# A bias table made in one fp32 matmul and one exponential, with first queries and keys ahead on SyncE's queue and every band row on it

## The chip, the cores and the metric

The kernel runs on one core of a Trainium2 chip. The metric is the device time of one execution in microseconds (us), the median of several runs. Engines are named as the profile names them: PE multiplies matrices, DVE and ACT do elementwise work (ACT also the exponentials), POOL and SP here issue transfers; PEld is PE's weight load.

## The reference

Attention with a learned bias by relative position, for 8 batches, 8 heads, 576 positions and 64 features, followed by a bilinear feed-forward layer over the 4608 tokens:

```
scores = q @ k.T / 8
n = abs(i - j)
bucket = n if n < 16 else min(31, 16 + int(log(n/16)/log(8) * 15))
scores += bias_table[bucket]          # 32 buckets x 8 heads
x = softmax(scores) @ v               # heads side by side: 4608 x 512
out = ((x @ w_a) * (x @ w_b)) @ w_out # 512 -> 1536 -> 512
```

Everything comes in and goes out in fp32.

## The kernel before

**The bias as a factor.** Softmax is unchanged when one value is subtracted from all scores of a head, so the kernel works with exp(bias − bias of the last bucket), which is 1 wherever two positions are at least 128 apart. The table in memory, `tab`, holds 1088 such factors for each head. It is filled with ones, and its middle 256 entries come from one matmul: `oh_sb`, a one-hot matrix of 32 buckets by 256 distances, against `eb_sb`, the exponentials of the differences in bf16 (line 250, after a subtraction on DVE in line 240). DVE copies the product into `tab_sb` (line 258) and SP sends it to `tab` (line 266). From there the band rows are read back as tiles, row after row shifted by one place: `W_sb` for each pair of heads, in two column parts (tokens `W0` to `W3` for columns from 320 on, `R0` to `R3` for the rest, line 261), and `Wt_sb` for the tail rows (`Wta`, `Wtb`). `W0` is issued by SP, the others by POOL. After its exponential each score tile is multiplied by its band on DVE (lines 470, 444, 539, 531).

**Pairs and stages.** Two heads make a pair; there are 32 pairs, four in each batch. 576 positions are four blocks of 128 and a tail of 64. For the first two batches (pairs 0 to 7) q and k are transposed on PE (lines 330, 339, 370) and copied out of PSUM to `QT`, `KT` and `ZB`; pairs 0 to 3 have their scores made in halves (line 455, `S`) with exponentials on ACT (line 461, `E`) and products on DVE (line 470, `M`). Later pairs use transposing transfers. `AV` are the products with v (lines 568, 572, 578), `N` their normalisation (lines 589 to 596), `X` the transposes of the result. Feed-forward units (`FA`, `FB`, `FO`: lines 642, 649, 652, 679) are put between them.

**The order.** The order in the opening, through the first feed-forward chunk, is a list of tokens written out by hand: `<` names are loads, `w2` is two filler matmuls on zeros, and the ending `:A` or `:D` says whether ACT or DVE does a copy or a padding. Every engine and every queue works through its instructions in this order. From pair 8 on a loop sets the order, which is the same for all the rest.

**The head.** Ahead of the list SP issues the constant `cn_sb` (one-hot matrix and identity), then q and k of the first pair in fp32 (`load_first`, line 226) into `kq32`, a part of `xn_sb` that is free until then. ACT issues two small loads of the bias table. The tokens `YQ` and `YK` turn the two fp32 pieces into bf16. POOL issues the other loads, which change the type on the way: `q123h0` is the first half of the positions of pairs 1 to 3, `q123h1` the second, `v0` and `v1` the values, `tq` and `tk` the tails of q and k, `vta` and `vtb` those of v, `wa0`, `wb0` and so on the weights.

```
nc.sync.dma_start(out=tab.ap(), in_=tab_sb[0:H, :])
...
load_w(int(name[1]), *((320, NY) if name[0] == "W" else (0, 320)), nc.sync if name in ('W0',) else nc.gpsimd)
```

Of the kernel before, what the change touches and what calls it, by code (L numbers as in the profile page):

```python
# [13 lines left out]
def kernel(  # L14
# [24 lines left out]
    NT = B * S  # L39
# [150 lines left out]
    def pad_z(b, hh):  # L190
        nc.vector.memset(ZB[b][64 * hh:64 * hh + 64, :, :, Dh - Dh * hh:128 - Dh * hh], 0.0)
# [45 lines left out]
    nc.vector.memset(tab_sb.bitcast(FP32)[0:H, :], TWO_ONES)  # L237
    pad_ones(0)
    pad_ones(1)
    nc.vector.tensor_tensor(out=bt_sb[0:NB, :], in0=bt_sb[0:NB, :], in1=bl_sb[0:NB, :],  # L240
                            op=mybir.AluOpType.subtract)
    warm = ps_av.tile([128, 512], FP32, tag="av", name="warm")

    def warm_up(n, dst=None):
        for _ in range(n):
            nc.tensor.matmul(out=(warm if dst is None else dst)[:, :], lhsT=zero_sb[:, 0:128],
                             rhs=zero_sb[:, :], start=True, stop=True)
# [12 lines left out]
    def load_w(hp, y0, y1, eng):  # L260
        eng.dma_start(out=W_sb[hp][:, :, y0:y1],
# [21 lines left out]
    def load(name):  # L283
        if name[0] in "qk" and name[1:2].isdigit():
            ps, _, half = name[1:].partition("h")
            p0, n = int(ps[0]), len(ps)
            if half:
                load_qh(2 * p0, 2 * p0 + 2 * n, int(half))
            else:
                b, h = divmod(2 * p0, H)  # L290
                (load_q if name[0] == "q" else load_k)(b, h, h + 2 * n)
        elif name[0] in "tu":
            load_compact(int(name[0] == "u"), int(name[1] == "k"))
        elif name in ("v0", "v1"):
            load_v(0, 4 * int(name[1]), 4 * int(name[1]) + 4)
        elif name[:3] == "vb1":
            load_v(1, *((0, 4) if name[3] == "a" else (4, 8)))
        elif name[:2] == "vt":
            load_vt_part(int(name[2] == "1"), "ab".index(name[-1]))
        elif name == "wo":  # L300
            load_w_out()
        elif name[:2] == "Wt":
            load_wt("ab".index(name[2]))
        elif name[0] in "WR":
            load_w(int(name[1]), *((320, NY) if name[0] == "W" else (0, 320)), nc.sync if name in ('W0',) else nc.gpsimd)
        else:
            load_weights(*((moe_w_a, wa_sb) if name[1] == "a" else (moe_w_b, wb_sb)), int(name[2]))

# [418 lines left out]
    def v_next(s):  # L727
# [7 lines left out]
    ACT = nc.scalar  # L735

    opening = """
        <q123h0 <k1 <tk <vtb <k23 <W1 <W0 <v0 <vta <tq <W2 <W3 <v1 <Wta <q123h1 <R0 <Wtb <R1 <k4 <wa0
        <wb0 <R2 <uq <q5 <q4 <R3 <k5 <wa1 <q7 <wb1 <k6 <uk <k7 <vb1a <vb1b <vt1a <q6 <wb2 <vt1b <wa2 <wo
        PC0:A PX0:D YQ0:A PC1:A PU0:D PV0:A PX1:D TQ0 YK0:D TK0 CQ00:A CQ01:D CK0:D TQ10 PF1:A CQ10:D  # L740
        S000 E000 PV1:D S001 E001 TK1 CK1:D TQ30 TZ1 CZ1:D S011 CQ30:D E011 S101 TQ20 CQ20:D E101 M101
        S100 E100 TK3 CK3:D KS EK M000 TK2 S301 E301 CK2:D w2 S200 E200 M100 M001 w1 S201 E201 V0:D
        PU1:D w2 S300 E300 M200 M201 AV00 TZ0 AV10 S010 CZ0:A N00 T0 N10 E010 X10 X00 CX00:A V1:D AV20
        CX10:A TQ11 TQ21 M301 M300 ET0 AV30 CQ11:A S110 CQ21:A N20 M010 M011 PW:A MT0 S111 TQ31 E110 X20
        CQ31:A E111 T1 ET1 N30 M110 X30 CX20:D CX30:D AV01 T2 TK4 M111 S210 ET2 E210 FA0a HA0a N01 T3
        MT1 X01 AV11 CK4:D CX01:A PF0:D LH ET3 N11 S211 E211 FB0a FA1a HA1a X11 G0a MT2 CX11:D S310 E310
        FB1a G1a S311 M210 FA2a FB2a HA2a E311 TQ5 TQ4 CQ4:A M211 FA3a AV21 CQ5:A S42 G2a S43 FB3a TZ0x
        MT3 M311 HA3a M310 TK5 E42 N21 FA4a HA4a CZ0x:D AV31 LV CK5:D X21 E43 TQ7 CQ7:A G3a N31 S41 E41
        S52 E52 FB4a FA5a HA5a CX21:D G4a M43 TK6 X31 CX31:D FB5a S40 E40 CK6:D S53 G5a FA0b HA0b TZ1x
        M41 CZ1x:D FB0b G0b S51 E53 FA1b HA1b TK7 FB1b FA2b E51 M52 HA2b CK7:D S50 G1b V2:D FB2b FA3b  # L750
        E50 V3:D G2b HA3b T4 M40 FB3b G3b S70 M42 ET4 MT4 FA4b FB4b T5 HA4b M53 E70 G4b TQ6 ET5 M51
        CQ6:A AV40 N40 FA5b S71 E71 S73 MT5 M50 FB5b HA5b AV41 S72 E73 G5b N41 M71 FA6f M73 T6 E72 M72
        ET6 MT6 AV50 FB6f HA6f N50 S62 S61 E62 G6f M62 FA7f HA7f AV51 N51 TH S60 E61 M61 FB7f G7f E60
        M60 S63 E63 FA8f HA8f T7 ET7 M63 M70 FB8f G8f AV60 FA9f FB9f N60 MT7 AV70 HA9f G9f FA10f HA10f
        FB10f N70 AV71 G10f FA11f HA11f FB11f N71 X71 AV61 X70 FO00 G11f N61 FO01 FO02 CX71:D CX70:D HO0
    """

    h0 = (0, 1)
# [2 lines left out]
    def step(token):  # L761
# [72 lines left out]
            tr_x(p, jqs)  # L834
        elif kind == "CX":
            copy_x(p, jqs, eng)
        elif kind == "YK":
            copy(eng, kn[0][:, 0:512], kq32[0])
        elif kind == "YQ":
            copy(eng, qn[0][:, 0:512], kq32[1])  # L840
        elif kind == "PV":
            pad_vt(0, p, eng)
        elif kind == "PC":
# [101 lines left out]
```

The softmax here doesn't subtract the row's maximum and nothing guards it: scores larger than these inputs give would overflow.

## Time and profile before

| what | value |
|---|---|
| time, median of 3 runs | 414.17 us (413.11 to 414.28) |
| the profiled execution, and its span from first to last instruction | 413.9 us, 412.1 us |
| PE busy | 401.5 us, 97% |
| DVE, ACT, POOL busy | 58%, 61%, 32% |
| chain that ended last, PE's share | 95% |

The page gives busy time by engine and, in forty slices of the span, how full each engine was. The times of the opening are read from the timeline, which lists start, length and the idle time ahead of each group of instructions with what ended it. A line of the profile reads: engine, line of the kernel, operation, output and input. The profile's lines are those of the kernel before; in the changed kernel the same statements stand five lines further up.

### The profile page before, as it was taken

Reading aid. Unit: us, or ns where it says so; the run is one execution under the profiler, and the core shown is the slowest. Engines: PE = TensorE matmul, PEld = TensorE weight load, DVE = VectorE, ACT = ScalarE, POOL = GpSimd, SP = SyncE. Lnnn points to the kernel's source line nnn. Section 1 sums busy time; section 2 is a strip of 40 time slices with the busy share of each in tenths; the row PEclk is TensorE's granted clock in tenths of the full one; section 3 lists DMA queues with packets and bytes.
Section 4 is the critical chain, followed back from the end, with each engine's and each line's share of the span. In section 5 each row is a group of like instructions: output and inputs, shape, how many; then the busy total and the mean of one; then the engine's idle time right before and its main releaser. Section 6 shows DMA issues by size and latency. Waiting matters only on the chain.

```text
span 412.1 us, 8718 instructions
## 1 busy us (share of the span) xinstructions
PE 401.5 (97%) x3420; PEld 209.6 (51%) x3471; DVE 240.6 (58%) x568; ACT 252.0 (61%) x386; POOL 131.4 (32%) x188
## 2 busy tenths in 40 slices
PE   7999999999999999999999999999999999999996
PEld 3476656455554555455445555555445454444443
DVE  4799997366755765476646764567547652421320
ACT  5898992577748665667557765767476642322321
POOL 5966466887029400960069004300000000000000
PEclk9999999999999999999999999999999999999999
DMA  9999999999969924994199908960520012002004
GB/s 152 185 204 197 206 137 148 166 184 131 91 127 157 141 40 91 151 127 94 35 159 150 120 17 136 117 92 17 117 67 17 16 40 78 0 5 98 2 2 102
DMA packets 135962, 42.36 MB, mean 103 GB/s; under 512 B 113544, under 2 KB 131176, under 8 KB 135920
## 3 DMA queue, kind: packets, MB, share of 16 engines
q0 software_dynamic: 81120, 19.88, 54.9%
q1 hardware_dynamic: 49456, 12.61, 19.9%
q10 hardware_dynamic: 5344, 9.31, 7.1%
q8 instruction: 27, 0.44, 0.5%
q14 instruction: 15, 0.12, 0.1%
HBM read 39.23 MB, written 9.45 MB: 118 GB/s over the span
## 4 chain that ended last, share of the span: by engine, by line
PE 95%; DMA 1%; ACT 1%; issue 1%; DVE 0%; ACTq 0%; SPq 0%
PE pb L642 23%; PE pa L642 23%; PE po L679 22%; PE av L578 8%; PE qk L415 7%; PE av L568 2%; PE av L572 2%; PE qkh L455 1%; PE qkt L488 1%; DMA xn<-in_k_dram 1%; PE trb L330 1%; PE trb L424 1%; PE trk L330 1%; ACT ath L461 0%; PE qkt L494 0%
## 5 line engine op out<-in xcount | busy, mean ns | idle before, releaser
L439 ACT ACTIVATE at<-qk 128x1024 bf16<-128x1024 f32 x112 | 113.4, 1029 | 27.4 <-DMA out_dram<-ob 10.3
L652 DVE TENSOR_TENSOR g<-pb,ha 128x512 bf16<-128x512 f32 (+1 forms) x114 | 75.6, 663 | 74.8 <-PE pb L642 58.5
L642 PE MATMUL pb<-xn,wb 128*128 128x512 bf16 (+1 forms) x440 | 111.1, 368 | 0.8
L642 PE MATMUL pa<-xn,wa 128*128 128x512 bf16 (+1 forms) x440 | 110.8, 368 | 0.7
L649 ACT ACTIVATE ha<-pa 128x512 f32<-128x512 f32 (+1 forms) x114 | 66.3, 581 | 67.6 <-PE pa L642 63.8
L679 PE MATMUL po<-wo,g 128*128 128x512 bf16 x403 | 95.5, 379 | 0.8
L444 DVE TENSOR_TENSOR at<-at,W 128x1024 bf16<-128x1024 bf16 x112 | 75.0, 685 | 22.4 <-ACT at L439 22.3
L642 PEld LDWEIGHTS <-wa 128*128 128x128 bf16 x456 | 41.2, 98 | 46.6 <-issue 6.8
L642 PEld LDWEIGHTS <-wb 128*128 128x128 bf16 x456 | 40.6, 98 | 42.9 <-issue 4.7
L679 PEld LDWEIGHTS <-g 128*128 128x128 bf16 x420 | 38.8, 98 | 44.9 <-issue 2.5
L684 ACT ACTIVATE ob<-po 128x512 f32<-128x512 f32 x34 | 20.4, 600 | 40.2 <-PE po L679 30.1
L578 PE MATMUL av<-vm,at 128*128 128x65 bf16 x896 | 41.2, 193 | 0.0
L578 PEld LDWEIGHTS <-at 128*128 128x128 bf16 x896 | 37.4, 97 | 6.1
L174 POOL DMA_DIRECT2D vt<-in_v_dram x12 | 7.4, 622 | 101.9 <-PE av L572 101.1
L136 POOL DMA_DIRECT2D qn<-in_q_dram x48 | 36.6, 825 | 9.2 <-PE trb L501 6.9
L589 DVE RECIPROCAL rc<-av 128x6 f32<-128x6 f32 (+1 forms) x64 | 11.9, 186 | 45.7 <-PE av L578 41.1
L145 POOL DMA_DIRECT2D kn<-in_k_dram x48 | 36.2, 800 | 2.6 <-DMA qn<-in_q_dram 1.6
L568 PE MATMUL av<-vt,att 128*128 128x130 bf16 x152 | 33.6, 221 | 0.2
L415 PE MATMUL qk<-QB,KB 64*128 64x512 bf16 x192 | 29.1, 381 | 0.3
L591 DVE TENSOR_TENSOR XG<-av,rc 128x384 bf16<-128x384 f32 (+2 forms) x64 | 27.2, 425 | 2.2
L515 ACT ACTIVATE att<-qkt 128x640 bf16<-128x640 f32 x24 | 16.8, 701 | 13.0 <-PE qkt L489 13.0
L568 PEld LDWEIGHTS <-att 128*128 128x128 bf16 x152 | 14.9, 98 | 6.4
(105 smaller groups left out, 322.8 us busy)
## 6 DMA issues: line engine op xcount, KB each, us to landing
out_dram<-ob ACTq DMA_DIRECT2D x31, 256.0 KB, 2.9
vn<-in_v_dram POOLq DMA_DIRECT2D x16, 256.0 KB, 5.7
kn<-in_k_dram POOLq DMA_DIRECT2D x48, 64.0 KB, 4.9
qn<-in_q_dram POOLq DMA_DIRECT2D x48, 64.0 KB, 4.1
wa<-in_moe_w_a_dram POOLq DMA_DIRECT2D x3, 512.0 KB, 8.9
wb<-in_moe_w_b_dram POOLq DMA_DIRECT2D x3, 512.0 KB, 8.3
wo<-in_moe_w_out_dram POOLq DMA_DIRECT2D x1, 1536.0 KB, 15.7
xn<-XG SPq DMA_TRANSPOSE x52, 3.5
```

The lines of the kernel that those rows point to most:

```text
L136: nc.gpsimd.dma_start(out=by_tile(qn[b % 2])[:, h0 // 4, t, :, :], in_=q[b, h0:h1, 128 * t:128 * t + 128, :].transpose([1, 0, 2]))
L145: nc.gpsimd.dma_start(out=by_tile(kn[b % 2])[:, h0 // 4, t, :, :], in_=k[b, h0:h1, t:SM:NM, :].transpose([1, 0, 2]))
L415: nc.tensor.matmul(out=ps[:, hh, :], lhsT=kT[r, t, :], rhs=qT[r, :, :], start=True, stop=True)
L439: nc.scalar.activation(out=at[:, :, :], in_=ps[:, :, :], func=ACTF.Exp, scale=scale)
L444: nc.vector.tensor_tensor(out=at[:, :, :], in0=at[:, :, :], in1=w[:, :, S - 1 + t:S - 1 + t - SM:-1], op=MULT)
L568: nc.tensor.matmul(out=pav[:, slot, :, :], lhsT=weights_tail(p, jq), rhs=vt[i][:, :, hp, :], start=True, stop=True)
L578: nc.tensor.matmul(out=pav[:, slot, hh, :], lhsT=weights(p, t, hh, jq), rhs=vm[i][:, 2 * hp + hh, t, :], start=False, stop=True, skip_grou ...
L591: nc.vector.tensor_tensor(out=xg[:, jqs[0]:jqs[0] + m, :, :], in0=pav[:, 0:m, :, 0:Dh], in1=rc[:, 0:m, :].unsqueeze(3).to_broadcast([128, ...
L642: nc.tensor.matmul(out=ps[:, 0:n], lhsT=w[df // 4][:, mc, 128 * (df % 4):128 * (df % 4) + 128], rhs=xn_sb[mc][:, 512 * c + lo:512 * c + lo ...
L649: nc.scalar.activation(out=ha[:, 0:n], in_=ff["pa", df, lo][:, 0:n], func=ACTF.Copy)
L652: nc.vector.tensor_tensor(out=g_sb[df][:, lo:lo + n], in0=ff["pb", df, lo][:, 0:n], in1=ff["ha", df, lo][:, 0:n], op=MULT)
L679: nc.tensor.matmul(out=po[:, :], lhsT=g_sb[df][:, 128 * tt:128 * tt + 128], rhs=wo_sb[:, df, :], start=(df == 0), stop=(df == NDF - 1))
```

## The change

- The differences to the last bucket go into the constant: a row of −1 is added to the one-hot matrix, so that one matmul of the raw bias table in fp32 gives bias minus last bias. The one-hot part is copied to fp32 on DVE (`oh32`, in a free part of `xn_sb`).
- The exponential is taken once, of the product, on ACT, straight into `tab_sb`. The second small load, the subtraction, `eb_sb` and the two fillers behind the table matmul are gone.
- SP issues q and k of the first pair first; the constant goes second on ACT's queue. Both type changes (`YQ`, `YK`) move ahead of the list, onto DVE.
- `W0` to `W3` all go on SP's queue.
- The list of the opening is a new one: loads in another order on POOL, copies and paddings divided otherwise between ACT and DVE, products with v and their neighbours in another order, one filler more.

```diff
+    oh_np[NB - 1, :] -= 1.0
...
-    oh_sb = cn_sb[:, 0:NR]
-    bl_sb = const.tile([128, H], FP32, name="bl_sb")
-    eb_sb = const.tile([128, H], BF16, name="eb_sb")
...
+    oh32 = xn_sb[2][:, NT - 512:NT].bitcast(FP32)
...
-    nc.sync.dma_start(out=cn_sb[:, :], in_=cn_handle.ap())
     load_first(q, kq32[1])
     load_first(k, kq32[0])
     nc.scalar.dma_start(out=bt_sb[0:NB, :], in_=bias_table)
-    nc.scalar.dma_start(out=bl_sb[0:NB, :],
-                        in_=bass.AP(tensor=bias_table.tensor, offset=(NB - 1) * H,
-                                    ap=[[0, NB], [1, H]]))
+    nc.scalar.dma_start(out=cn_sb[:, :], in_=cn_handle.ap())
...
-    nc.vector.tensor_tensor(out=bt_sb[0:NB, :], in0=bt_sb[0:NB, :], in1=bl_sb[0:NB, :],
-                            op=mybir.AluOpType.subtract)
+    pad_z(0, 0)
+    pad_z(0, 1)
+    nc.vector.tensor_copy(out=oh32[0:NB, :], in_=cn_sb[0:NB, 0:NR])
...
     warm_up(5)
-    nc.scalar.activation(out=eb_sb[0:NB, :], in_=bt_sb[0:NB, :], func=ACTF.Exp)
-    nc.tensor.matmul(out=tps[0:H, 0:NR], lhsT=eb_sb[0:NB, :], rhs=oh_sb[0:NB, :],
+    nc.tensor.matmul(out=tps[0:H, 0:NR], lhsT=bt_sb[0:NB, :], rhs=oh32[0:NB, :],
                      start=True, stop=True)
-    warm_up(2)
-    pad_z(0, 0)
-    pad_z(0, 1)
-    nc.vector.tensor_copy(out=tab_sb[0:H, c0:c0 + NR], in_=tps[0:H, 0:NR])
+    nc.vector.tensor_copy(out=qn[0][:, 0:512], in_=kq32[1])
+    nc.scalar.activation(out=tab_sb[0:H, c0:c0 + NR], in_=tps[0:H, 0:NR], func=ACTF.Exp)
+    nc.vector.tensor_copy(out=kn[0][:, 0:512], in_=kq32[0])
...
-... nc.sync if name in ('W0',) else nc.gpsimd)
+... nc.sync if name in ('W0', 'W1', 'W2', 'W3') else nc.gpsimd)
```

The head of the list, before and after:

```diff
-        <q123h0 <k1 <tk <vtb <k23 <W1 <W0 <v0 <vta <tq <W2 <W3 <v1 <Wta <q123h1 <R0 <Wtb <R1 <k4 <wa0
-        <wb0 <R2 <uq <q5 <q4 <R3 <k5 <wa1 <q7 <wb1 <k6 <uk <k7 <vb1a <vb1b <vt1a <q6 <wb2 <vt1b <wa2 <wo
-        PC0:A PX0:D YQ0:A PC1:A PU0:D PV0:A PX1:D TQ0 YK0:D TK0 CQ00:A CQ01:D CK0:D TQ10 PF1:A CQ10:D
-        S000 E000 PV1:D S001 E001 TK1 CK1:D TQ30 TZ1 CZ1:D S011 CQ30:D E011 S101 TQ20 CQ20:D E101 M101
-        S100 E100 TK3 CK3:D KS EK M000 TK2 S301 E301 CK2:D w2 S200 E200 M100 M001 w1 S201 E201 V0:D
-        PU1:D w2 S300 E300 M200 M201 AV00 TZ0 AV10 S010 CZ0:A N00 T0 N10 E010 X10 X00 CX00:A V1:D AV20
+        <q123h0 <tk <k1 <k23 <W0 <W1 <v0 <W3 <W2 <Wtb <vtb <tq <vta <q123h1 <R1 <Wta <v1 <R0 <R2 <k4
+        <wa0 <wb0 <q4 <q7 <k7 <q5 <vt1b <R3 <k5 <wa1 <uq <uk <wb1 <vb1a <vb1b <k6 <vt1a <wb2 <q6 <wa2
+        <wo PF1:D PU1:A TQ0 CQ00:A TK0 PX1:D PX0:D PU0:A PV1:D CK0:D PC0:A PF0:A CQ01:D w1 S000 E000
+        TQ10 S001 TK1 CQ10:D TZ1 E001 CK1:D S011 E011 TQ30 PV0:D S101 E101 CQ30:D CZ1:D TK3 CK3:D TK2
+        CK2:D V0:D S100 E100 TQ20 CQ20:D S301 E301 w2 S200 E200 w2 KS EK w1 S300 M101 S201 E300 TZ0
+        CZ0:A M000 E201 M100 AV10 M001 AV00 M301 TQ11 CQ11:A M200 T0 M300 N10 X10 N00 PW:D ET0 TQ31
+        CQ31:A M201 S010 E010 S110 E110 CX10:D TQ21 V1:D LH M011 X00 CX00:A M010 CQ21:A AV20 AV30 S111
```

More of the change, by code (lines that the diff above doesn't have):

```diff
@@ L304, in load @@
         elif name[0] in "WR":
-            load_w(int(name[1]), *((320, NY) if name[0] == "W" else (0, 320)), nc.sync if name in ('W0',) else nc.gpsimd)
+            load_w(int(name[1]), *((320, NY) if name[0] == "W" else (0, 320)), nc.sync if name in ('W0', 'W1', 'W2', 'W3') else nc.gpsimd)
         else:
@@ L743 @@
-        PU1:D w2 S300 E300 M200 M201 AV00 TZ0 AV10 S010 CZ0:A N00 T0 N10 E010 X10 X00 CX00:A V1:D AV20
[L744 to L752, printed above, removed]
@@ L753 @@
-        ET6 MT6 AV50 FB6f HA6f N50 S62 S61 E62 G6f M62 FA7f HA7f AV51 N51 TH S60 E61 M61 FB7f G7f E60
-        M60 S63 E63 FA8f HA8f T7 ET7 M63 M70 FB8f G8f AV60 FA9f FB9f N60 MT7 AV70 HA9f G9f FA10f HA10f
-        FB10f N70 AV71 G10f FA11f HA11f FB11f N71 X71 AV61 X70 FO00 G11f N61 FO01 FO02 CX71:D CX70:D HO0
+        <q123h0 <tk <k1 <k23 <W0 <W1 <v0 <W3 <W2 <Wtb <vtb <tq <vta <q123h1 <R1 <Wta <v1 <R0 <R2 <k4
+        <wa0 <wb0 <q4 <q7 <k7 <q5 <vt1b <R3 <k5 <wa1 <uq <uk <wb1 <vb1a <vb1b <k6 <vt1a <wb2 <q6 <wa2
@@ new lines @@
+        E111 T1 N20 X20 MT0 AV01 N30 CX20:D M110 N01 ET1 X30 MT1 TK4 M111 T2 CX30:A S210 FA0a X01 ET2
+        HA0a CX01:D FB0a E210 MT2 G0a CK4:A T3 AV11 N11 FA1a ET3 HA1a TQ4 M210 S211 E211 FB1a X11 CX11:A
+        FA2a HA2a S311 G1a CQ4:D S310 E311 FB2a MT3 FA3a HA3a E310 M211 TK5 G2a M311 TQ5 CK5:A PC1:D
+        AV21 N21 S42 M310 S43 FB3a FA4a G3a CQ5:A X21 TZ0x AV31 LV E42 CX21:D TQ7 N31 CZ0x:D HA4a FB4a
+        G4a S41 E43 M43 S52 FA5a CQ7:A TK7 E41 X31 CX31:D S40 HA5a E52 CK7:D E40 FB5a G5a V2:D FA0b HA0b
@@ new lines @@
+        S53 FB0b M42 TZ1x TK6 G0b E53 CZ1x:D M53 FA1b HA1b S51 E51 FB1b G1b FA2b M40 V3:D S50 FB2b HA2b
+        E50 G2b FA3b M41 HA3b T4 ET4 FB3b G3b S70 CK6:D MT4 FA4b FB4b T5 TQ6 AV40 HA4b M50 M52 G4b E70
+        S71 ET5 N40 FA5b FB5b MT5 CQ6:A E71 HA5b M51 AV41 N41 S72 G5b S73 E72 M72 FA6f E73 AV50 M70 M73
+        N50 S62 FB6f T6 HA6f E62 M62 ET6 FA7f HA7f G6f MT6 AV51 N51 TH S61 S60 E61 M61 E60 FB7f G7f S63
+        E63 M60 M63 FA8f M71 T7 FB8f HA8f G8f AV60 N60 ET7 MT7 FA9f HA9f FB9f G9f AV70 FA10f FB10f N70
@@ L756 @@
+        HA10f G10f AV71 FA11f FB11f HA11f N71 X71 AV61 X70 FO00 FO01 G11f FO02 N61 CX70:D CX71:D HO0
     """
@@ L836, in step @@
             copy_x(p, jqs, eng)
[L837 to L840, printed above, removed]
         elif kind == "PV":
```

## The prediction

> **What bounds the kernel now.** I read the page first. Its table of forty slices gives PE a 7 in the first slice and 9 in every one until the last.
>
> ```profile
> PE   7999999999999999999999999999999999999996
> ```
>
> So a change at the head can only win what PE loses there, and it must be kept by a PE that never pauses again. Busy PE counts pipelined ends, so I went next to the busy time by stretches, cut where the opening changes its character.
>
> ```profile
> 0.00:7.90 7.90, 5.28 (x32) 1.88 (x32) 3.95 (x19) 3.94 (x8) 3.78 (x9) 1.00 0.97 157
> 7.90:19.50 11.60, 11.09 (x117) 5.52 (x119) 8.06 (x19) 9.79 (x11) 11.04 (x16) 1.00 1.09 174
> 19.50:25.30 5.80, 5.08 (x109) 4.05 (x106) 5.44 (x15) 5.46 (x12) 4.63 (x7) 1.00 1.27 212
> 25.30:40.00 14.70, 14.70 (x227) 10.95 (x226) 13.27 (x44) 13.09 (x21) 9.49 (x13) 1.00 1.39 196
> ```
>
> The columns are PE, PEld, DVE, ACT, POOL. From 25.3 us PE has no gap (14.70 of 14.70). Before that come three stages: a start to 7.9, a stretch to 19.5 in which PE and ACT are both nearly full, and one to 25.3 in which DVE (5.44 of 5.80) and ACT (5.46) lead. The chain of waits, in order of time, names what the first two hang on:
>
> ```profile
> 1.72 4.51 DMA xn<-in_k_dram
> 6.25 0.44 DVE kn L322
> 6.73 0.68 PE trk L330 x8
> 7.43 0.44 DVE KT L322
> 7.92 1.03 PE qkh L455 x8
> ...
> 15.33 0.63 PE warm L246
> 15.96 0.54 PE qkh L455 x4
> ```
>
> The first keys' transfer alone is 4.51 us of the start; then the chain runs through PE itself, warm-up fillers included. The ACT timeline shows what PE's pace costs there:
>
> ```profile
> 8.57 1.94 ACT L461 ACTIVATE ath<-qkh 128x1024 bf16<-128x1024 f32 x2 [1.97 <-PE qkh L455]
> 10.67 2.86 ACT L461 ACTIVATE ath<-qkh 128x1024 bf16<-128x1024 f32 x3 [0.17 <-PE qkh L455]
> 13.93 1.02 ACT L480 ACTIVATE atk<-qkt 128x1024 bf16<-128x1024 f32 x1 [0.40 <-PE qkt L476]
> 16.55 2.95 ACT L461 ACTIVATE ath<-qkh 128x1024 bf16<-128x1024 f32 x3 [0.48 <-PE qkh L455]
> ```
>
> Ten exponentials of about 0.93 us fill 8.57 to 19.50 (10.93 us), 1.6 us of it idle, before scores that PE had not made.
>
> **What the Trainium skill says.** "TensorE: Matmul & The Clock Gate", Part 1, What's actually happening: the array runs at half clock until about 3.4 us of sustained work. The trace agrees in kind, though not in the waiting time: fillers of 512 columns start 0.43 us apart at 2 us, score groups still take half-rate steps (0.18 to 0.21 us for 256 columns) at 17.1, and the two fillers at 17.45 are 0.23 apart. The granted clock stands at 1.00 throughout, so it doesn't show this. "FP8 and Floating Point Precision", TensorE Precision Notes: true fp32 takes four passes. No fp32 matmul is in this trace. "DMA: Bandwidth & Descriptors", Issuing engines are not separate DMA queues: all issuers share the engines, and more of them save issue time only. The trace agrees: the q transfer landed 3.19 us after issue nearly alone, the k transfer behind it, beside POOL's loads, took 4.51.
>
> **Part 1, head of SyncE's queue: −1.0 us.** SP issued the constant at 0.74, q at 1.18, k at 1.72. Now q goes at 0.74 and k at 1.18, 0.54 earlier; the constant (96 KB) goes second on ACT's queue. From k's landing to the first exponential the trace has 8.57 − 6.23 = 2.34 us (cast 0.44, eight transposes 0.68, copy 0.44, scores to exponential 0.65, steps between). With the same 4.51 us k lands at 5.7 (gain 0.5); with q's 3.19, at 4.4. Of the three first transfers one is now on another queue, but the bytes up to the last of k are about the same, so I take 5.2: gain 1.0, bounds 0.5 and 1.3. Nothing else must lie in the way. DVE's new padding between the cast and the key copy is 0.27 + 0.11 + 0.11 + 0.28 = 0.77, as long as the transposes it waits for. ACT must do four paddings of about 0.4 and one q copy before the first exponential; from a table exponential ending near 5.0 that reaches 7.0, before the scores (7.5). The one filler ahead of the scores (0.43) lies inside the key copy.
>
> **Part 2, the table: +0.6 us, hidden.** Before: subtract 3.18, exponential 3.37, matmul 3.63, cast 4.04 to 4.45, transfer issued 4.48, seen by its waiters at 7.80. Removed: one small load, the subtract, the fold of the exponential into a bf16 operand. Added: an fp32 copy of the one-hot differences, 32x256, which waits for the constant (landed 2.16 us after issue before; now issued near 1.2, so about 3.6), about 0.3 by the 64x256 copies; the matmul, four passes, estimated from the page and half rate at 4 × 0.21 = 0.85, less if the passes are fewer (0.21); the exponential out of PSUM, about 0.35. So 3.6 + 0.3 + 0.8 + 0.35 = 5.05 against 4.48, bounds 4.5 and 5.6. PE's queue holds the q transposes behind that matmul, and DVE's the q and k casts behind the copy; both are ready only at 4.4 and 5.2, so the wait costs nothing unless the constant lands after 4.7. The two fillers that followed the table matmul are gone; they ran in idle time.
>
> **Part 3, band rows on SP.** The table is seen at 8.4; four issues of 0.39 go at 8.4, 8.8, 9.2, 9.6. By the single SP transfer of before (2.58) plus contention, the second lands at 11.4 to 12.0. The first product that needs it was at 12.64, and now stands behind two key copies, the values' copy and a q copy, at about 12.0. So nothing is lost, with little to spare. POOL issues three loads fewer (0.73 each). After five loads it still waits once for the table (3.24 before, some 3.5 now), with the v tails (which landed at 7.67 and will at about 13; the first value product needs them after 17), the q tails and the second q half behind that wait. The values now pass ahead of that wait: issued near 4.2 instead of 8.77, so their copy can run at 11 instead of 16.05, in DVE's idle time.
>
> **Part 4, the order.** In the score stretch PE is at half rate. Steps from the timeline: 0.48 a score group, 0.57 eight transposes of keys, 0.35 of a q half, 0.22 tails, 0.96 tail scores, 0.43 a filler. From the first score group through the last of this stage the new order has nine groups (4.32), three key sets (1.71), three q halves (1.05), one set of tails (0.22), the tail scores (0.96) and five fillers (2.15), 10.41 together. The old order has the same counts, with some gaps and the last group at full rate, and took 10.39 (7.92 to 18.31). The first part's 1.0 is kept: the last scores are out at 17.3 instead of 18.3.
>
> Then ACT: from the tenth exponential to the end of the second pair's last half it had 6.4 us; a copy of 0.33 and the tail-table copy of 0.42 go to DVE, the rest keeps its length. ACT ends that half at about 24.25 against 25.91, −1.65. DVE, step by step from the product that needs the eighth exponential (17.9): eight products at 0.60, four first normalisations at 0.55, three copies at 0.25 to 0.33, a tail pair at 0.56, one long normalisation at 0.98 and 0.2 for the tail table end near 25.9, or 26.5 with the one product that the old order has ahead of this point. There it was 27.70: −1.2, and −1.3 one tail pair later. DVE is the later of the two, so −1.3 is what reaches PE. After 25.3 PE has no idle; ACT receives about 1.2 us of copies more in 25 to 38, where its gaps were about 1.4. I charge nothing, bound 0.6.
>
> Sum: 412.1 − 1.3 = 410.8 of span. The three runs have a median of 414.17 (the profiled execution, 413.9, lies 1.8 above its span), so 412.9. The runs spread 1.17 us, and 0.3%, about what a measurement of this kernel can tell from no change, is 1.24.
>
> **Rivals.**
> *The clock rises earlier.* PE is closer packed from 6.9 on, so full rate may come at 13 to 14 instead of 17.4. The last six items (3.7 us) would halve; ACT's 0.93 a step then limits, and about 1.0 more is won: 411.9. Against it: PE was nearly gapless from 11.3 to 17.4 and stayed slow.
> *The gain is absorbed.* The bytes before k's last packet are the same, so k lands at 5.7; or the second band transfer lands late and holds the products on a DVE that is full from then on. Then 0.5 or less: 413.9.
> *Slower: POOL's queue behind the table.* The second q half is the fourth load behind the one that waits for the table, so issued near 11.2 (8.4 + 4 × 0.72), against 13.64 before, where it took 6.05. In the new order its transposes stand in PE's queue right after the first two value products, at about 18.8, and all later scores behind them. Four band transfers (520 KB) now share the engines with it. From a landing at 18.8 each microsecond costs one; from 21.4 (a latency of 10.2, where 8.9 is the longest seen below 30 us) the sum exceeds +1.3: 415.5.
>
> That the compiled order differs from the diff is excluded by the instruction lists of both kernels.
>
> **How the numbers follow.** Main case 0.42, of which 0.27 beyond 0.3%; earlier clock 0.23; absorbed 0.20; slower 0.13, and 0.02 for what I haven't seen. Faster 0.27 + 0.23 = 0.50; same 0.15 + 0.20 = 0.35; slower 0.15. The range runs from the earlier clock with the best landing (411.3) to the absorbed case plus half of the slower one (414.9).
>
> **What would show it.** Right: k landing near 5.2, first exponential near 7.5, table transfer issued near 5.05, last first-stage scores at 17.3, gapless PE from about 24, all later lines shifted by 1.3. Wrong: full-rate fillers before 15, PE waiting for the second q half, a first product after 12.6, or PE gaps between 25 and 40 before copies on ACT.

## The result and the profile after

The changed kernel takes 417.12 us (median of 6 runs, 416.1 to 418.91), the kernel before 413.94 (6 runs, 413.11 to 414.28): a ratio of 1.0086, 95% interval 1.0062 to 1.011. The forecast was 412.9, range 411.3 to 414.9: it had the wrong sign, by 4.2 us. The profiled execution of the changed kernel took 417.26 us, its span is 415.5 (before: 413.9 and 412.1). Ahead of the table's transfer the lines of the two kernels differ by one to four, from there on by five. Figures of single loads below are issue and landing in the trace; each comes from one profiled execution.

The page's row of slices shows it coarsely: two 9s have become 7s, in the second and third slices (10.4 to 31.2 us). The chain that ended last says more: 8% of it now is DMA and 88% PE, where PE had 95% before.

```profile
PE   7779999999999999999999999999999999999996
...
PE 88%; DMA 8%; issue 1%; POOL 1%; ACT 1%; ACTq 0%; DVE 0%
```

The busy time by stretches (PE, PEld, DVE, ACT, POOL, granted clock, DMA share, GB/s), for the same four stretches as before:

```profile
0.00:7.90 7.90, 5.67 (x36) 2.01 (x36) 4.11 (x19) 3.54 (x8) 4.06 (x9) 1.00 0.97 167
7.90:19.50 11.60, 9.36 (x114) 4.83 (x112) 8.13 (x17) 9.23 (x11) 7.55 (x12) 1.00 1.08 161
19.50:25.30 5.80, 5.43 (x116) 4.37 (x113) 5.01 (x17) 5.55 (x10) 5.59 (x8) 1.00 1.05 168
25.30:40.00 14.70, 12.87 (x198) 9.60 (x196) 11.93 (x35) 12.15 (x21) 8.37 (x12) 1.00 1.31 184
```

The start is better (5.67 of PE instead of 5.28). Then PE lacks 1.7 us up to 19.5 and 1.8 between 25.3 and 40, where it had been full. POOL, which only issues transfers, falls from 11.04 to 7.55 in the second stretch. The first `po` product, where the last step of the first feed-forward chunk begins, starts at 74.51 instead of 71.03; from there to the end both kernels need the same (340.94 and 341.07). So everything happens in the opening. What PE waited for there, longest first (total, times, longest):

```profile
PE pb L637 <- DMA wb<-in_moe_w_b_dram: 2.1, 2, 1.8
PE trb L365 <- DMA tlc<-in_q_dram: 1.3, 1, 1.3
```

Two loads, the q tails and the second weights; PE waited for no load after 7 us before. The chain of waits up to 32 us, in order of time, says why they were late:

```profile
1.23 2.93 DMA cn_sb<-cn_const
...
4.18 0.29 DVE xn L238
...
4.51 1.03 PE tab_ps L248 x2
...
5.57 0.38 ACT wo L252
...
5.97 3.71 DMA bias_tab<-wo
9.68 0.28 issue
9.96 0.62 POOL Wt L264
10.59 6.89 DMA vt<-in_v_dram
17.48 0.29 issue
17.77 0.72 POOL W L256
...
19.43 0.74 POOL wa L274
20.17 9.79 DMA wb<-in_moe_w_b_dram
```

It is the making of the table from end to end, and then POOL's queue: constant, fp32 copy, fp32 matmul, exponential (`wo` is the memory that `tab_sb` lies in), the table's transfer, POOL's load of a tail band that reads the table, then the loads behind it. POOL's timeline has both its stops, with their lengths in brackets:

```profile
4.18 0.93 POOL L126 DMA_DIRECT2D vn<-in_v_dram  x1
9.96 0.63 POOL L264 DMA_DIRECT2D Wt<-bias_tab  x1 [4.86 <-DMA bias_tab<-wo]
...
17.77 0.72 POOL L256 DMA_DIRECT2D W<-bias_tab  x1 [1.75 <-DMA vt<-in_v_dram]
```

The first stop is the wait for the table (3.24 before). The second: the issue at 17.77 follows the landing, at 17.48, of the v tails issued at 10.59, the eighth load before it; eight of POOL's loads were in flight. While SP and POOL both stood, the transfer engines ran dry. The stretch 9 to 11 us in single microseconds, last two columns DMA share and GB/s; first the changed kernel, then the kernel before, whose own dip is shorter and earlier (36 GB/s from 8.5 to 9.0 us):

```profile
9.00:10.00 1.00, 1.00 (x18) 0.51 (x16) 0.69 (x2) 0.72 (x2) 0.04 (x1) 1.00 0.14 23
10.00:11.00 1.00, 1.00 (x18) 0.53 (x18) 0.69 (x3) 1.00 (x2) 1.00 (x2) 1.00 0.13 23
```

```profile
9.00:10.00 1.00, 1.00 (x21) 0.76 (x23) 0.41 (x1) 1.00 (x2) 1.00 (x2) 1.00 0.81 191
10.00:11.00 1.00, 1.00 (x12) 0.42 (x8) 0.75 (x4) 0.83 (x2) 1.00 (x3) 1.00 0.87 110
```

Thirteen loads were then issued from 9.70 to 15.24 in one burst (the thirteen from 7.80 on took until 15.64 before), and most of them took longer: q tails 11.19 to 18.44 (before 10.14 to 14.09), v tails 10.59 to 17.48, second q half 12.48 to 19.63 (before 13.64 to 19.68), second weights 20.17 to 29.97 (before 18.33 to 26.60). ACT's timeline shows that the first part of the change did what it was meant to, and where its gain goes:

```profile
7.75 1.93 ACT L456 ACTIVATE ath<-qkh 128x1024 bf16<-128x1024 f32 x2
9.95 1.94 ACT L456 ACTIVATE ath<-qkh 128x1024 bf16<-128x1024 f32 x2 [0.28 <-PE qkh L450]
...
16.63 1.02 ACT L456 ACTIVATE ath<-qkh 128x1024 bf16<-128x1024 f32 x1
18.81 0.77 ACT L315 ACTIVATE ZB<-trb 64x256 bf16<-64x256 bf16 x2 [1.17 <-PE trb L365]
```

The first exponential is at 7.75 instead of 8.57, 0.82 ahead; the tenth ends at 20.6 instead of 19.5, behind the tails for which PE waited.

### The profile page after: what moved, and what is told of

The parts are those of the page before. It is cut to its first block, busy times and chain, and to the rows that moved or that the text cites. A ratio compares the mean times of both kernels' runs of the same rounds, so it can differ in the third digit from the quotient of the medians.

```text
span 415.5 us, 8711 instructions
## 1 busy us (share of the span) xinstructions
PE 401.2 (97%) x3420; PEld 210.0 (51%) x3471; DVE 240.8 (58%) x568; ACT 251.5 (61%) x385; POOL 129.2 (31%) x185
## 3 DMA queue, kind: packets, MB, share of 16 engines
q1 hardware_dynamic: 50128, 12.91, 19.5%
## 4 chain that ended last, share of the span: by engine, by line
PE 88%; DMA 8%; issue 1%; POOL 1%; ACT 1%; ACTq 0%; DVE 0%
PE pb L637 22%; PE pa L637 22%; PE po L674 22%; PE qk L410 7%; PE av L573 7%; DMA wb<-in_moe_w_b_dram 4%; PE av L563 2%; DMA vt<-in_v_dram 2%; PE av L567 2%; PE qkt L483 1%; DMA bias_tab<-wo 1%; DMA cn_sb<-cn_const 1%; PE trb L419 1%; POOL wa L274 0%; POOL tlc L161 0%
```

## The experiments

The theories, by their letters in the expectations. A: the table's later time stops POOL, and all loads behind it come late. B: the new list is itself too eager. C: the bands on SP crowd POOL's loads. D: the earlier first scores count for more than the table. E: the table's transfer stands in the transfer engines behind loads that POOL issued ahead of it. Ratios are to the kernel before, timed beside it on the same chip (medians there 413.26 to 413.86). A difference between two variants is one of medians, partly from different chips. "Seen" is the time at which SP issues the first band load, which waits for the table.

| kernel | edit | us (runs) | ratio (95%) | table issued, seen |
|---|---|---|---|---|
| before | | | | 4.48, 7.80 |
| after | all of it | 417.12 (6) | 1.0086 (1.0062 to 1.011) | 5.97, 9.70 |
| e1_head | new head, old list | 414.32 (14) | 1.0016 (1.0008 to 1.0025) | 6.45, 9.23 |
| e2_bands_sp | before + bands on SP | 414.76 (18) | 1.0020 (1.0005 to 1.0035) | 4.47, 8.05 |
| e3_list_only | old head, new list, bands on SP | 415.83 (6) | 1.0049 (1.0033 to 1.0064) | 4.97, 9.22 |
| e7_list_pool | old head, new list, bands on POOL | 418.39 (6) | 1.0122 (1.0102 to 1.0143) | 4.45, 8.76 |
| e8_order_only | before + order of first transfers | 416.01 (6) | 1.0050 (1.0034 to 1.0066) | 7.08, 9.36 |
| e4_late_wt | after, tail band later on POOL | 415.21 (20) | 1.0045 (1.0030 to 1.0059) | 6.04, 10.40 |
| e6_cq7 | e4, one ACT copy earlier | 415.43 (7) | 1.0051 (1.0031 to 1.0071) | 5.83, 10.73 |
| e5_cn_first | after, constant first on SP | 414.67 (15) | 1.0028 (1.0018 to 1.0037) | 5.05, 9.44 |
| e9_v0_behind | after, values behind the tail band | 417.76 (4) | 1.0099 (1.0079 to 1.0119) | 6.09, 8.30 |
| e10_tails_ahead | after, tails ahead of the tail band | 415.52 (6) | 1.0057 (1.0035 to 1.0080) | 5.91, 10.69 |
| e11_cn_v0 | e5 and e9 | 417.96 (4) | 1.0109 (1.0089 to 1.0128) | 5.06, 8.72 |
| e15_cn_v0_late | e11, values' copy later | 416.43 (6) | 1.0086 (1.0057 to 1.0115) | 5.06, 8.73 |
| e16_v0_late | e9, values' copy later | 416.96 (5) | 1.0078 (1.0063 to 1.0093) | 5.86, 8.83 |
| e12_fill | before + two fillers | 414.00 (14) | 0.9998 (0.9987 to 1.0008) | 4.45, 7.77 |
| e13_before_nowait | before, bands from a constant | 413.75 (13) | 1.0003 (0.9992 to 1.0014) | no wait |
| e14_after_nowait | after, bands from a constant | 413.88 (13) | 1.0005 (0.9995 to 1.0015) | no wait |
| e17_nowait_s41 | e14, scores moved near 37 us | 413.65 (14) | 1.0003 (0.9992 to 1.0014) | no wait |
| e18_cn_s41 | e5, the same move | 414.98 (6) | 1.0044 (1.0026 to 1.0061) | 5.05, 9.43 |

### The parts, one at a time

`e1_head` takes the new head with the old list and the old queues of the bands. `YQ0` and `YK0` go from the list, since the head does them; against the kernel before, beside the lines of the head:

```diff
-        PC0:A PX0:D YQ0:A PC1:A PU0:D PV0:A PX1:D TQ0 YK0:D TK0 CQ00:A CQ01:D CK0:D TQ10 PF1:A CQ10:D
+        PC0:A PX0:D PC1:A PU0:D PV0:A PX1:D TQ0 TK0 CQ00:A CQ01:D CK0:D TQ10 PF1:A CQ10:D
```

> The changed head alone (fp32 table, first queries and keys first, both casts on DVE) with the old list, bands on the queues of before. Theory A (the later table holds POOL's queue, and what stands behind it comes late): table transfer issued near 6.0, POOL waits 4.8 us in place of 3.2, first scores 0.8 earlier but the loads behind the wait 1.5 later; 1.0 to 2.5 us slower than before. Theory B (the new list asks for loads earlier than they can come): no slower than before, up to 0.8 faster. Theory C (four band transfers on SP crowd POOL's loads out): the same as B.

414.32: the head costs 0.5 where the list stays, between what A (1.0 to 2.5) and what B and C (nothing) expected. POOL waits 4.67 for the table, nearly the changed kernel's 4.86, yet the loads behind that wait take about as long as before (q tails 11.56 to 15.97), and PE waits for none of them. Its first exponential is at 9.37: ACT's paddings of the old list now stand behind the table's exponential (6.05).

`e2_bands_sp` is the kernel before with the four band issues on SP.

```diff
-... nc.sync if name in ('W0',) else nc.gpsimd)
+... nc.sync if name in ('W0', 'W1', 'W2', 'W3') else nc.gpsimd)
```

> The kernel before with the four band transfers on SP's queue and nothing else changed. Theory A: POOL no longer waits at the first band and issues values, v tails and q tails 3 us earlier, its wait for the table moves to the tail table when that has long landed; 0 to 1 us faster. Theory B: within 0.5 us of before. Theory C: the loads issued beside the bands take 6 to 7 us in place of 4, 1 to 3 us slower.

414.76. With no band in front, POOL runs on to the second values before it waits, for 0.81. The bands pay for it; SP's timeline, and the wait on DVE:

```profile
4.47 0.35 SPq L266 DMA_DIRECT2D bias_tab<-wo  x1
8.05 2.34 SPq L261 DMA_DIRECT2D W<-bias_tab  x4
```

```profile
DVE ath L470 <- DMA W<-bias_tab: 2.2, 1, 2.2
```

The first two bands take 6.3 us or more (landed 14.39, 15.29; W0 took 2.6 before) and the first product waits 2.2. That is Theory C turned round: the bands, not POOL's loads, are late. That POOL's freed loads crowd them is argued, not tested.

`e3_list_only` and `e7_list_pool` put the new list behind the old head (with `YQ0:D YK0:D` at its start), the one with bands on SP, the other with only `W0` there.

```diff
-        <wo PF1:D PU1:A TQ0 ...
+        <wo YQ0:D YK0:D PF1:D PU1:A TQ0 ...
```

> The new list and all bands on SP with the head of before (bf16 table, constant first on SP), both casts on DVE at the head of the list. Theory A: table transfer issued at 4.5, POOL's wait about 3.3, the wait for the q tails falls from 1.3 to 0 and that for the second weights from 1.8 to below 0.5; 2 to 3.5 us faster than the changed kernel, about the time of before. Theory B and C: both waits stay over 1 us, within 1 us of the changed kernel.

> The new list alone: head of before (both casts on DVE at the head of the list), and the bands 1 to 3 issued by POOL as before, so that POOL stands at the band before the values. Theory B (the list itself is too eager): the ACT copy near 40 us and the wait for weights stay, 1.5 to 2.5 us slower than before. If the list is slow only together with the bands on SP: within 0.7 us of before.

415.83 and 418.39. So the list alone costs 2.0 with the bands on SP and 4.5 with them on POOL: the bands on SP repair part of what the new list would cost. The head alone (0.5) and the list with its bands (2.0) don't add up to 3.2; the rest comes only where they meet. In both the table was issued no later than 4.97, yet seen 4.3 us on (3.3 before): the new list issues the k loads of pairs 2 and 3 by 3.42 us, where before two small tail loads stood between and the last went at 4.03, and e3 the values at 4.18 as well. That is the first sign for Theory E. With the bands on POOL, PE waits 1.2 us for the second weights.

`e8_order_only` gives the kernel before the order q, k on SP, constant first on ACT, to see what the earlier scores bring by themselves.

```diff
-    nc.sync.dma_start(out=cn_sb[:, :], in_=cn_handle.ap())
     load_first(q, kq32[1])
     load_first(k, kq32[0])
+    nc.scalar.dma_start(out=cn_sb[:, :], in_=cn_handle.ap())
     nc.scalar.dma_start(out=bt_sb[0:NB, :], in_=bias_table)
```

> The kernel before with q and k at the head of SP's queue and the constant at the head of ACT's, table in bf16 and list as before. Keys land 0.8 earlier, the constant near 3.3, the table transfer near 5.0 in place of 4.5, POOL's wait 0.5 longer. Theory A: between 0.3 slower and 0.5 faster than before. Theory D: 0.7 us faster than before.

416.01, but not for Theory D: the 1 KB load `bl_sb`, now third on ACT, took 3.96 us instead of 1.89. The subtraction waited for it, then the exponential and the matmul (PE stood 2.7 us), and the first exponential of scores slid to 10.11. It tells how a tiny load fares behind large ones, and nothing of D.

### The wait in POOL's queue

`e4_late_wt` moves the tail band that stops POOL behind five other loads; `e6_cq7` is e4 with the query copy `CQ7` right behind its transposes, since PE waited for that copy near 40 us.

```diff
-... <v0 <W3 <W2 <Wtb <vtb <tq <vta <q123h1 <R1 <Wta <v1 <R0 <R2 <k4
+... <v0 <W3 <W2 <vtb <tq <vta <q123h1 <v1 <Wtb <R1 <Wta <R0 <R2 <k4
```

```diff
-... TQ7 N31 CZ0x:D HA4a FB4a G4a S41 E43 M43 S52 FA5a CQ7:A TK7 ...
+... TQ7 CQ7:A N31 CZ0x:D HA4a FB4a G4a S41 E43 M43 S52 FA5a TK7 ...
```

> The changed kernel with the first tail-table load moved on POOL's queue from sixth place to behind v tails, q tails, second q half and second values; head, list of compute and bands as changed. Theory A: POOL does not wait early, the q tails land before 12 and the first feed-forward weights about 3 us earlier; PE's waits for both vanish; 3 to 4.5 us faster than the changed kernel, 0 to 1.5 faster than before. Theory B: the wait for the second weights stays, at most 1.5 faster than the changed kernel. Theory C: the bands, still together on SP, keep the loads at 6 to 7 us, at most 1 us faster than the changed kernel.

> The kernel with the late tail-table load (e4_late_wt), and in it one ACT copy of transposed queries moved in the list from behind the sixth feed-forward half unit to directly behind its transposes, as in the list of before. If the place of that copy made PE wait 0.77 and 0.23 us near 40 us, these go and the time falls by 0.7 to 1.0 us against e4_late_wt, to 414.3; if the wait is only moved, under 0.3.

e4 wins back 1.9 of 3.2 (415.21). No PE wait for tails or weights is left, as A has it, but A expected 3 or more: the bands now land at 14.7 to 18.1, and a product waits 2.2. Its executions also split by their mean granted clock: the eleven at 0.998 or more have a median of 414.66, the nine below it 416.04. In e6 (415.43) PE's wait moved from the copy to an exponential (1.02 at 40.7) and nothing was won.

`e10_tails_ahead` moves only the three tail loads ahead of the wait.

```diff
-... <v0 <W3 <W2 <Wtb <vtb <tq <vta <q123h1 ...
+... <v0 <vtb <tq <vta <W3 <W2 <Wtb <q123h1 ...
```

> The changed kernel with v tails and q tails issued ahead of the tail-table load, so that PE's wait for the q tails (1.31) must go, and only the second q half and what follows stay behind the table. If that wait and the limit of loads in flight behind the tails were the cost: 1.5 to 3 us faster than the changed kernel. Theory E says that the table comes later still, near 10.5, with products waiting for bands: at most 1.5 us faster.

415.52. The wait for q tails is gone; the table, behind three loads more, is now seen 4.8 us after its issue. In the profiled execution, which was the slowest of its six (417.96), PE waits 1.9 for a normalisation instead, until 21.6, and around its end the granted clock (third number from the end) falls to half, until 28.2:

```profile
21.40:28.20 6.80, 6.64 (x86) 5.22 (x87) 5.37 (x17) 4.35 (x7) 3.93 (x6) 0.50 1.29 203
```

The four executions whose mean granted clock is 0.998 or more took 415.1 to 415.6, the other two 417.0 and 418.0.

`e5_cn_first` issues the constant first on SP, as before, and leaves the rest.

```diff
+    nc.sync.dma_start(out=cn_sb[:, :], in_=cn_handle.ap())
     load_first(q, kq32[1])
     load_first(k, kq32[0])
     nc.scalar.dma_start(out=bt_sb[0:NB, :], in_=bias_table)
-    nc.scalar.dma_start(out=cn_sb[:, :], in_=cn_handle.ap())
```

> The changed kernel with the constant back at the head of SP's queue, q and k behind it; fp32 table, list and bands as changed. Theory A (the table's time gates POOL and all behind it): the constant lands near 2.9 in place of 4.2, the table transfer goes at 4.9 to 5.1 in place of 6.0, first scores 0.8 later; 0.7 to 1.5 us faster than the changed kernel. Theory D (the first scores count more than the table): 0.5 to 1 us slower than the changed kernel.

414.67, 2.45 below the changed kernel and the lowest of the variants that keep its list and read the table. SP's timeline:

```profile
5.05 0.35 SPq L261 DMA_DIRECT2D bias_tab<-wo  x1
9.44 1.92 SPq L256 DMA_DIRECT2D W<-bias_tab  x4
```

That is more than A expected (0.7 to 1.5), and the opposite of what D did (0.5 to 1 slower). The constant lands at 2.83 instead of 4.16 and the table is issued 0.92 earlier, but it is seen only 0.26 earlier, 4.4 us after its issue. The first exponential is back at 8.82, so the loads behind the wait have 1.07 us more before they are needed. They also take less: q tails 5.70 instead of 7.25, and POOL's second stop is 0.43 long instead of 1.75. No PE wait for a load is left. Why the same burst, 0.3 us earlier, drains so much better, the profiles don't say. Nor is the constant's place the whole of it: e3 has the constant first as well, with the same list of loads and its table issued and seen even a little earlier (4.97, 9.22), and still loses 2.0.

### The table's transfer

`e9_v0_behind` puts the first values behind the waiting load, so that the table has less in front of it; `e11_cn_v0` does so with the constant first as well.

```diff
-... <W0 <W1 <v0 <W3 <W2 <Wtb <vtb ...
+... <W0 <W1 <W3 <W2 <Wtb <v0 <vtb ...
```

> The changed kernel with the first values' load moved on POOL's queue from ahead of the tail-table load (where POOL waits for the table) to right behind it; all else as changed. Theory E (the table's transfer queues in the DMA engines behind what POOL has issued before it, so the values ahead of it make the table late whatever the time of its issue): table seen by its waiters at 8.3 to 8.8 in place of 9.7, POOL's wait 3.5 to 4, all loads behind it about 1 us earlier; 0.8 to 2 us faster than the changed kernel. Theory A alone (only the time of issue counts): table still seen near 9.5, no faster, up to 0.5 slower.

> Both mends together: constant first on SP (as in e5_cn_first) and the values' load behind the tail-table load (as in e9_v0_behind). Theory E: table issued at 5.05 and seen near 8.0, as in the kernel before (7.8); 413.5 to 414.2 us, level with the kernel before. Theory A alone: as e5_cn_first, 414.7.

In e9 the table is seen 2.2 us after its issue, SP's timeline:

```profile
6.09 0.36 SPq L261 DMA_DIRECT2D bias_tab<-wo  x1
8.30 1.93 SPq L256 DMA_DIRECT2D W<-bias_tab  x4
```

With one 256 KB load less ahead of it the same 17 KB took 2.2 instead of 3.7; in e16, which has the same loads in the same order, 3.0, and with the constant first 3.7 (e11, e15) instead of 4.4 (e5, e18). So Theory E holds in direction, though e11's table, expected near 8.0, came at 8.72, and the same order can differ by 0.8 from one execution to the next. The time did not follow (417.76; e11 417.96), because the values now landed at 16.07 instead of 9.53, and their copy stands on DVE in front of the first products. DVE's wait and, through it, PE's in e9:

```profile
DVE vm L317 <- DMA vn<-in_v_dram: 3.7, 1, 3.7
```

```profile
PE qkh L450 <- DVE QT L317: 2.6, 1, 2.6
```

`e15_cn_v0_late` and `e16_v0_late` therefore move that copy, in e11 and e9, to where the first product with v needs it.

```diff
-        CK2:D V0:D S100 E100 ...
-        CZ0:A M000 E201 M100 AV10 M001 ...
+        CK2:D S100 E100 ...
+        CZ0:A M000 E201 M100 V0:D AV10 M001 ...
```

> The kernel with constant first and values behind the tail-table load (e11_cn_v0), and in its list the copy of the first values moved on DVE from ahead of the first products to ahead of the first value product. If the early copy of late values was what held DVE (and PE 2.43 us behind it): that wait goes, 2.5 to 3.5 us faster than e11_cn_v0, 414.5 to 415.5. If the bands or tails come too late anyway: less than 1.5.

> The same move of the values' copy, with the head of the changed kernel (constant on ACT's queue): e9_v0_behind with the copy later. If first scores 0.8 earlier are worth something once nothing else waits: 0.3 to 0.8 faster than e15_cn_v0_late; if the table's issue at 6.0 decides: level or slower.

416.43 and 416.96, better by 1.5 and 0.8 than e11 and e9, still far from e5. In e16 PE waits 3.3 us for the q tails, in spite of a table seen 0.9 us earlier than in the changed kernel, and the granted clock is at half right behind that wait:

```profile
19.10:22.50 3.40, 3.31 (x50) 3.12 (x51) 2.34 (x8) 2.17 (x4) 3.40 (x6) 0.50 1.22 201
```

Neither an earlier issue alone nor a faster transfer alone frees the loads: every order pays for one load with another.

### Without the wait

`e12_fill` adds two fillers to the kernel before, to see whether its clock could rise earlier: `TQ0 w2 YK0:D TK0`.

> The kernel before with two more fillers on PE between the first q transposes and the first key transposes, where PE idles 1.0 us. If the array's clock rises with closely packed work, full rate comes before 16 in place of 17.4 and the score stage, paced by PE at half rate, gains 0.5 to 1.2 us against before. If the time of the rise doesn't depend on this idle time: within 0.3 us of before.

414.00, no difference, though full rate did come earlier in the profiled execution: two fillers at 16.77 are 0.23 apart, where before one at 16.44 still took its half-rate step and 17.45 was the first such pair.

`e13_before_nowait` and `e14_after_nowait` read all bands from a constant of ones in memory. The table is still made and written, but nobody waits for it; the bias is left out of the result.

```diff
+    tabc = nc.inline_tensor(np.ones((H, TB), dtype=ml_dtypes.bfloat16), name="tab_const")
...
-                          in_=bass.AP(tensor=tab, offset=2 * hp * TB + y0,
+                          in_=bass.AP(tensor=tabc, offset=2 * hp * TB + y0,
```

> The kernel before with its bands read from a constant of ones, so that no load waits for the table (which is still made and written, but not used: the bias is left out of the result). It is the partner of e14_after_nowait. POOL then never stands still; values land near 10 in place of 13. If the table's wait costs anything in the kernel before: 0.5 to 1.5 us faster than before.

> The changed kernel with its bands read from a constant of ones, no wait for the table's landing (the table is still made and written, but not used: the bias is left out of the result); SP's band loads still go behind the table's issue, near 6.3. If the table's wait is the cause of the loss: all of 3.2 comes back and the 1.3 forecast appears, 1 to 1.5 us faster than e13_before_nowait or level with it. If the list's own order is slow: still 1.5 to 2.5 us slower than e13_before_nowait.

This pair decides. The kernel before wins nothing when its wait of 3.24 us goes: 413.75 without, 413.66 with it on the same chip. (That is a net sum: its first exponential then comes at 9.07, 0.5 later.) The changed kernel falls to 413.88, 3.2 below 417.12, its whole loss. But it is not faster than before either. The stretches and PE's waits from 7 us on in e14:

```profile
7.90:19.50 11.60, 10.75 (x153) 6.30 (x149) 9.04 (x23) 10.79 (x14) 8.35 (x13) 1.00 1.27 208
19.50:25.30 5.80, 5.59 (x117) 4.45 (x111) 5.68 (x18) 5.28 (x10) 2.78 (x5) 1.00 1.30 203
25.30:40.00 14.70, 13.91 (x199) 10.00 (x196) 12.74 (x38) 12.09 (x20) 9.67 (x14) 1.00 1.40 199
```

```profile
PE trb L326 <- ACT QT L316: 0.8, 1, 0.8
PE qkh L451 <- ACT atk L476: 0.6, 1, 0.6
PE trb L614 <- ACT QT L316: 0.3, 1, 0.3
PE qk L411 <- ACT at L435: 0.2, 1, 0.2
```

First scores are early (7.69), loads are in time, and PE is fuller from 19.5 to 25.3. But it waits for ACT at 16.2, 19.1, 39.3 and 40.3 us, 1.84 together, where the kernel before has two such waits, 0.72 together. Near 39 us ACT itself stands 2.37 before the copy for which PE then waits. The starts of PE's `pa` units show where the lead goes. The first is at 25.44 instead of 27.40 and the fifth at 34.39 instead of 36.75, both more than 1.9 ahead; the seventh is at 41.03 instead of 41.84, the eighth at 42.99 instead of 43.47. About 1 us of that is the two waits at 39.3 and 40.3; the two lists also put other work between the units.

`e17_nowait_s41` and `e18_cn_s41` fill that gap in e14 and e5 with scores made earlier.

```diff
-... X21 TZ0x AV31 LV E42 ... G4a S41 E43 M43 S52 FA5a CQ7:A TK7 E41 X31
+... X21 TZ0x S41 AV31 LV E42 ... G4a E43 M43 E41 S52 FA5a CQ7:A TK7 X31
```

> The changed kernel with its bands read from a constant of ones (bias left out of the result), and with the second scores of pair 4 made ahead of the last product with v (AV31) and their exponential ahead of the query copy CQ7, so that ACT, idle for 2.37 us at 36.3 to 38.7 us, has work. Theory L (the early gain is given back by the list near 39 us, where PE waits 0.76 and 0.23 us): the two waits shrink to 0.3 or less together and the time falls by about 0.7, to 413.2. Theory M (the wait only moves, as it did when the copy alone was moved): PE waits about 1 us elsewhere between 36 and 50 us and the time stays at 413.9.

> The changed kernel with the constant first on SP, and the same move. Theory L: 414.67 minus about 0.7, so 414.0, level with the kernel before; PE waits near 41 us down from 0.66 to 0.3 or less. Theory M: 414.7, with the wait elsewhere.

413.65 and 414.98: within what the runs can tell, no gain. The waits became one of 0.65 in e17 (from 0.99) and one of 0.97 in e18 (from 0.66). So the place near 39 us is where a loss shows, and filling ACT's gap there did not recover it.

## Why the prediction was wrong, point by point

**What bounds the kernel.** One reading is off: the lengths of the ten exponentials from 8.57 to 19.50 add up to 9.8 us, which leaves 1.1 us idle, not 1.6. And the view's granted clock of 1.00 "throughout" is no statement about the opening: the trace's own records of it begin at 17.31 us in the kernel before and at 14.52 in the changed one, just where the fillers go to full rate.

**Part 1** held. k was forecast to land at 5.2 and landed at 5.32, the first exponential near 7.5 and came at 7.75.

**Part 2** is where it begins: "the table: +0.6 us, hidden", 5.05 for the issue of its transfer, with 5.6 as the worst. It was 5.97. Of the 0.92 on top, 0.56 is the constant (landed 4.16, forecast 3.6, as the second load on ACT's queue beside q and k), 0.23 the fp32 matmul (1.03 instead of 0.8), the rest exponential and steps. The Trainium skill, "FP8 and Floating Point Precision", TensorE Precision Notes, gives four passes for fp32; the trace doesn't show four but two matmul records for it, 1.02 us together, against 0.37 for the bf16 one before, so the size is near what I took. That "the wait costs nothing unless the constant lands after 4.7" was right for PE (the keys were cast by 5.77 and their transposes began at 5.89) and asked after the wrong waiter: the queue that mattered was POOL's.

**Part 3 is the step that failed**: "The table is seen at 8.4", that is 3.3 us after issue as before, with POOL's wait "some 3.5" and "nothing is lost, with little to spare". It was seen at 9.70, 3.73 after issue, and POOL stood 4.86. I had counted as a gain that "the values now pass ahead of that wait"; they also pass ahead of the table. In the trace the table's eight packets move between 8.8 and 9.3 us (6.8 to 7.3 before), together with the last packets of the k and v loads that POOL had issued, and e9 and e16 bear it out: 2.2 and 3.0 us with the values behind. I had quoted the Trainium skill, "DMA: Bandwidth & Descriptors", Issuing engines are not separate DMA queues, to price q and k, and not to the table's transfer, where it applied as well; the trace agrees with it there. The second band landed at 14.66, not at 11.4 to 12.0, and the first product came at 14.76, not at about 12.0 (12.64 before):

```profile
14.76 1.90 DVE L465 TENSOR_TENSOR ath<-ath,W 128x1024 bf16<-128x1024 bf16 x3 [1.61 <-DMA W<-bias_tab]
```

That there is no loss without the wait is shown by e14 (3.2 of 3.2 us back). The wait alone is not the loss either: e1 has 4.67 of it and loses 0.5, and under its old list PE waits for no load. It takes the wait together with the new list (e3: 4.52 of wait, 2.0 lost), which issues the values ahead of the table and asks for the q tails ahead of the first product with v. The constant's new place is worth 2.45 of the 3.2 in e5, through two things at once, a slightly earlier table and a later need; as e3 loses 2.0 with the constant first, how the loss divides is not shown. The dry stretch of the engines with the burst behind it, and the stop at eight loads in flight, are read from the trace and were not tested alone; e1 has a stretch as dry (19 GB/s and less from 8.5 to 10.0 us) and its q tails then take 4.4.

**Part 4** failed as well, at "I charge nothing, bound 0.6" for the time after 25 us. Its sum for DVE doesn't come out as written: the pieces add up to about 9.6 us, which from 17.9 gives 27.5 and not 25.9. Yet with the wait out of the way (e14) DVE ended that normalisation at 25.52, against 27.70 before, so the gain was there at this point, and nothing of it reaches the end. PE's waits for ACT in e14 exceed those of before by 1.1, the longest near 39 us, where the lead of the `pa` units goes; that the list's division of copies makes them is argued from this and not shown, since the moves tried (e6, e17, e18) only shifted them. This stays open.

**The rivals.** The slower one, POOL's queue behind the table, was the mechanism, at a chance of 0.13 and with the wrong load: the second q half, which I had watched, landed at 19.63; the q tails (18.44) came to PE's turn first, and the second weights cost most. I followed one load to the end where I should have followed all those behind the wait to their first use. The earlier clock: fillers at the full-rate spacing of 0.23 do come at 14.6, instead of 17.4, and it brought nothing, as PE then waited for loads. It brought nothing in e14 either, where no PE wait for a load is left: there two fillers at 14.08 are 0.23 apart.

## What to carry to other kernels

When a change lengthens the chain to something that a queue waits for, list every transfer behind that wait with the time of its first use, and price the wait by the earliest that fails. Here a wait of 4.7 to 4.9 us cost 0.5 under the old list and 3.2 under the new one (e1 and the changed kernel). A load moved ahead of a short, urgent transfer is not free: here the values ahead of it made the table 0.7 to 1.5 us later (e9 and e16 against the changed kernel, e11 against e5). And an earlier start is worth only what the stages behind it can take: here, with the wait removed, 0.8 us at the first scores was worth nothing at the end.

## What the runs showed that I had not expected

- A 17 KB transfer from SP was seen by its waiters 2.2 to 4.9 us after issue (e9, e6), in the main later the more of POOL's loads had been issued ahead; the 1 KB load third on ACT's queue took 3.96 us instead of 1.89 (e8).
- The kernel before hides a wait of 3.24 us on POOL altogether (e13, ratio 1.0003, 0.9992 to 1.0014); its list hides most of 4.67 too (e1); 4.86 with other loads behind it cost 3.2.
- The granted clock was at half again for 6.8 us behind a PE wait of 1.9 (e10) and for 3.4 behind one of 3.3 (e16). PE waits of 2.6 (e9) and 2.4 (e11) fell ahead of the first rise, which came near 20 us in both. That is one profile each, and that the waits cause it is not tested; if they do, a late load costs more than the wait for it.
- The rise itself was at 14.5 us in the changed kernel's profile and at 8.8 in e16's, though PE's work is the same in both up to then. Nor is a lower mean clock slower as such: of 130 executions of the kernel before, the 31 with a mean below 0.995 have a median of 412.94, the others 413.86. No trace of one of those 31 was kept.
- POOL stopped with eight of its loads in flight (17.77 us, after the landing at 17.48 of the eighth before).
- Putting the bands on SP is worth 2.6 us under the new list (e7 to e3) and costs 0.9 under the old one (e2).
- An fp32 matmul of 32 by 8 by 256 took 1.02 us in the half-rate opening, as two records, against 0.37 in bf16.
